# Batch 1's attention wholly inside unit 0, and batch 2's q^T by DMA transposes

## The chip, the cores and the metric

The kernel runs on one core of one Trainium2 chip. The metric is the device time of one execution in microseconds (us), lower is better. The kernel before took 335.55 us (median of 3 runs, 335.01 to 336.0). Where a text says "path", it means the instructions of TensorE (PE) in their order, since PE issues in order and nearly fills the span.

## What is computed

Per batch (8) and head (8) there are 1024 rows of 64 numbers. A Linformer attention is followed by a feed-forward layer with the larger of two products:

```python
k_proj = einsum('ks,bhsd->bhkd', E, k); v_proj = einsum('ks,bhsd->bhkd', F, v)   # 1024 -> 64 rows
attn = softmax(q @ k_proj^T / 8); x = attn @ v_proj        # per batch and head
x = x.transpose(0, 2, 1, 3).reshape(8192, 512)
out = maximum(x @ w1, x @ w2) @ w_out                      # 512 -> 1024 -> 512, float32
```

The inputs are float32 and are cast to float16 by the loads.

## The kernel before, in words

**Units.** Each batch makes two units of the feed-forward work, numbered 0 to 15. A unit has an "up" part (line 558, seven products p1, p2, p6, p5, p7, p3, p4 for each half of the features) and a "down" part (line 636, seven products of the same names). The matrices are multiplied in seven products of half size in place of eight, with sums and differences of operands made by VectorE (DVE): `step_s` (line 519) makes those of x and of g, `sub4` (line 475) those of the weights. A product that is kept is copied out of PSUM by `keep` (line 529), in unit 0's down part by DVE and elsewhere by ScalarE (ACT); `add` (lines 573 and 660) adds two of them.

**Order.** All instructions are in an order written out by hand. `slots` is a list of keys with a piece of work each, and `at_slot` hangs further steps behind a key. Batch 0's up part comes first (line 404); then unit 0's down part alone, in 14 pieces of 6 matmuls with keys ("P", 0, product, half). A list of 15 strings says which attention steps of batch 1 follow the pieces: string n stands behind piece n, and string 0 behind key (0, 19), ahead of the pieces. From unit 1 on, the down part of unit n and the up part of unit n + 1 alternate: some pieces of down, then key ("G", n, 0), some more pieces, then the up products ("U", n, 0, 0) to ("U", n, 0, 6) with a piece of down between each two; then the same with ("G", n, 1) and ("U", n, 1, i).

**Attention.** `step_kv` (line 180) projects k and v, ACT and DVE copy the results; `step_kpt` (line 211, copy on line 216) transposes k_proj on PE. q^T is made in one of two ways. `step_qt` (line 237) makes eight 128x128 transposes on PE, and DVE copies them out of PSUM in one instruction (line 242). `step_qt_dma` (line 249) has SyncE's DMA queue (SP) do it, 16 tiles a call. A batch has four groups (g, j): g is one of two sets of four heads, j one of two halves of the rows. A group's steps are the scores (`sc`, line 266, 16 small matmuls) with the exponential on ACT, the sums (`dn`, line 278, 8 matmuls) with a logarithm on ACT, the inverse (`in`, ACT) and the values (`at`, line 278, 16 matmuls), whose DVE multiplications write x^T (line 329 or 381). In unit 0 a group's steps are placed one by one. Later groups go through `step_group` (from line 333): behind key ("G", n, h) stand the sums and values of one group and the scores of the next.

**PSUM.** Unit 0's down part uses banks 0 and 1. The attention in unit 0 uses banks 2 and 3 by turns (`mm_bank`) for q^T and values, and two pairs of banks (`att_banks`) by turns for scores, sums and k_proj^T. `step_at` with `att=True` takes such a pair in place of banks 2 and 3. The up part of later units uses banks 2 and 3, too, and so do the scores in `step_group`.

**Loads.** k, v and q of a batch are loads of 1 MB each, which GpSimd's queue (POOL) issues in order into four buffers. A load waits on POOL until its buffer is free, and all behind it wait, too. `step_gate` (line 229) is a 1x1 copy on POOL which reads the result of a DMA transpose, so that the loads behind it on POOL start only once this has landed. Outputs are stored from four `o_sb` buffers by SP (line 651), in order with the DMA transposes.

**Batches before the change.** Of batch 1, the groups (0,0) and (1,0) and the scores of (0,1) are placed in unit 0; the group (0,1)'s sums and values and (1,1)'s scores stand behind ("G", 1, 0), (1,1)'s sums and values behind ("G", 1, 1). Batch 2's `step_kv` stands behind ("U", 1, 0, 1), its `step_kpt` behind ("U", 1, 0, 4), and four `step_qt` behind later up products of unit 1. Batches 3 to 7 use `step_qt_dma` at ("G", n, 0), a DMA transpose of k_proj, and the gate.

Of the kernel before, what the change touches and what calls it, by code (L numbers as in the profile page):

```python
# [16 lines left out]
def kernel(  # L17
# [14 lines left out]
    B, H, S, D = q.shape  # L32
# [27 lines left out]
    def mm_bank(dtype=FP32, n=None):  # L60
        if n is None:
            n = turn.pop(0)
            turn.append(n)
        return ps.tile([128, 512 if dtype == FP32 else 1024], dtype, tag=f"mm{n}", name="mm_ps")

    def att_banks(dtype=FP32):
        return ps.tile(
            [128, 2, 512 if dtype == FP32 else 1024], dtype, tag="att", bufs=2, name="att_ps"
        )
# [6 lines left out]
            name=nc.get_next_instruction_name(),  # L76
# [20 lines left out]
    def load_all(t, b, n, src):  # L97
        alloc(t, n)
        load(t, n, src, b, 0, H)
# [7 lines left out]
    tiles = {b: {} for b in range(B)}  # L107
# [180 lines left out]
    def values_into(t, g, j, at_ps):  # L288
        for z in range(2):
            tiles_into(  # L290
                lambda o: at_ps[o][:, z * W : (z + 1) * W], t["ex", g, j],
                lambda rows, hh: t["vp"][rows, 4 * g + hh, z, :],
            )

    def new_xt(t):
        t["xt"] = xpool.tile([128, NP2, 2, HALF], FP16, tag="xt", name="xt_sb")

    def x_out(t, g, j):
        return t["xt"][:, 2 * g : 2 * g + 2, :, j * W : (j + 1) * W]
# [15 lines left out]
        ld = t["ld", g, j]  # L315
        nc.scalar.activation(out=ld, in_=ld, func=ACTF.Exp, scale=-1.0)

    def step_at(t, g, j, att=False):
        if "xt" not in t:
            new_xt(t)  # L320
        ld = t.pop(("ld", g, j))
        if att:
            both = att_banks()
            at_ps = [both[:, o, :] for o in range(2)]
        else:
            at_ps = [mm_bank() for _ in range(2)]
        values_into(t, g, j, at_ps)
        for o in range(2):
            nc.vector.tensor_tensor(
                out=x_out(t, g, j)[:, :, o, :],  # L330
                in0=at_ps[o].rearrange("q (z n) -> q z n", z=2),
                in1=ld[:, o, None, :].broadcast_to([128, 2, W]),
                op=ALU.mult,
            )
# [121 lines left out]
    U = {(b, o): {"n": n, "b": b, "o": o, "t": tiles[b]} for n, (b, o) in enumerate(units)}  # L456
# [260 lines left out]
    t = tiles[0]  # L717
# [25 lines left out]
    step_dn(t, 1, 0)  # L743
    step_inv(t, 1, 0)
    step_at(t, 0, 0)
    step_dn(t, 1, 1)
    step_inv(t, 0, 1)
    step_kv(t, 4, 8, "v")
    step_inv(t, 1, 1)
    step_at(t, 1, 0)  # L750
    step_wd(0)

# [6 lines left out]

    def loads(b, *names):  # L760
        for n in names:
            b_ = b + (n == "k" and b < 3)
            if b_ < B:
                load_all(tiles[b_], b_, n, {"k": k, "v": v, "q": q}[n])

    slots = [
        (0, u0[0]), (None, f(step_at, 0, 1)), (1, u0[1]), (None, f(step_at, 1, 1)),
        (None, lambda: loads(1, "v", "q", "k")),
        (None, wd[1]), (2, u1[0]), (3, u1[1]), (4, u0[2]), (None, wt[0]), (5, u0[3]),
        (None, wd[2]), (None, wt[1]), (6, u1[2]), (7, u1[3]), (8, u0[4]), (9, u0[5]), (None, wd[3]),  # L770
# [30 lines left out]
    def at_slot(key, s, *a):  # L801
        steps.setdefault(key, []).append(lambda: s(*a))
# [11 lines left out]
    t = tiles[1]  # L814
    at_slot((0, 19), new_attn, t)
    at_slot((0, 19), lambda: turn.__setitem__(slice(None), [2, 3]))
    for n, x in enumerate((
        "kv", "", "kpt", "qt00 qt10", "", "sc00 sc10", "qt01", "qt11", "",
        "dn00 in00 dn10 in10", "", "", "at00 AT10 sc01", "", "",
    )):  # L820
        key = ("P", 0, (n - 1) // 2, (n - 1) % 2) if n else (0, 19)
        for name in x.split():
            if name[0] == "k":
                if name == "kpt":
                    at_slot(key, step_kpt, t, 0, H, True)
                else:
                    at_slot(key, step_kv, t)
                    at_slot(key, loads, 2, "v", "q")
            else:
                g, j = int(name[2]), int(name[3])  # L830
                s_ = {"qt": step_qt, "sc": step_sc,
                      "dn": step_dn, "in": step_inv, "at": step_at, "AT": step_at}[name[:2]]
                args = (4 * g, 4, 2 * j, 2 * j + 2) if name[:2] == "qt" else (g, j)
                at_slot(key, s_, t, *args, *([True] if name[:2] == "AT" else []))
                if name == "qt11":
                    at_slot(key, loads, 2, "k")
        if n in (1, 5):
            at_slot(key, step_t, 1, (0, 1) if n == 1 else (2, 3))
        if 6 <= n < 10:
            at_slot(key, sums_x, U[0, 1], ((2, 0, 1, 3)[n - 6],))  # L840


    t = tiles[2]
    at_slot(("P", 0, 6, 0), new_attn, t)
    at_slot(("U", 1, 0, 1), step_kv, t, 0, H, "kv", True)
    at_slot(("U", 1, 0, 1), loads, 3, "q", "v")
    at_slot(("U", 1, 0, 4), step_kpt, t, 0, H, True)
    for i, key in enumerate((("U", 1, 0, 5), ("U", 1, 1, 1), ("U", 1, 1, 3), ("U", 1, 1, 5))):
        at_slot(key, step_qt, t, 4 * (i % 2), 4, i // 2 * 2, i // 2 * 2 + 2, True)
    for b in range(3, B):  # L850
        t = tiles[b]
        n = 2 * b - 3
# [3 lines left out]
        at_slot(("U", n, 0, 1), step_kv, t, 0, H, "kv", True, True)  # L856
        at_slot(("U", n, 0, 6), step_gate, t)
        at_slot(("U", n, 0, 6), loads, b + 1, "k", "v", "q")
    groups = [(tiles[b], g, j) for b in range(1, B) for j in range(2) for g in range(2)][2:]
    none = (None, None, None)  # L860
    for i, (new, old) in enumerate(zip([*groups[1:], none], groups)):
        n, h = divmod(i + 2, 2)
        if new[0] is not None:
            at_slot(("G", n, h), lambda t=new[0], h=h: t.__setitem__("first", (h, 1 - h)))
        at_slot(("G", n, h), step_group, *new, *old)
        at_slot(("U", n, h, 0), step_later)
        at_slot(("U", n, h, 2), step_later)
# [59 lines left out]
```

## Time and profile before

| what | value |
|---|---|
| time of the profiled execution | 335.55 us |
| its span, first to last instruction | 333.8 us |
| median of the runs (3) | 335.55 us |
| lowest, highest | 335.01, 336.0 us |
| PE busy | 320.1 us (96%) |
| DVE busy | 242.2 us (73%) |
| ACT busy | 201.3 us (60%) |
| POOL busy | 37.0 us (11%) |
| granted PE clock, mean | 0.994 |

All times of instructions are us from the start of the span. A row of the timeline has the start, the time from the first start to the last end of the row, the engine, the line, what is written from what, and how many; in brackets stands the engine's idle time before it and what ended it. Matmuls are pipelined, so a row of them overlaps the next: a row's cost on the path is the distance from its start to the next row's start.

Where things stand in the span: unit 0's down part runs from 54.2 to 68.1, unit 1 from 68.1 to about 91, and from about 111.5 on each batch takes some 36 us.

### The profile page before, as it was taken

To read this page: it belongs to the slowest core of one execution; us is meant where nothing else is said; L and a number is where in the kernel's file an instruction comes from. 1 tells how busy PE (TensorE), PEld (TensorE's weight loads), DVE (VectorE), ACT (ScalarE), POOL (GpSimd) and SP (SyncE) were. 2 spreads that over 40 slices of the span, in tenths; PEclk is the share of its full clock that TensorE was granted. 3 is DMA by queue.
4 is the path that set the end of the run, shared out by engine and by line. 5 is a ranking of instruction groups with operands and counts; after the bars stand their busy time and mean duration, and the time that the engine had idled before them with its cause. 6 is when DMAs were issued, how large, how long until landed. Compare 5 with 4: busy or idle time off the path is not lost.

```text
span 333.8 us, 9067 instructions
## 1 busy us (share of the span) xinstructions
PE 320.1 (96%) x3884; PEld 250.2 (75%) x3884; DVE 242.2 (73%) x428; ACT 201.3 (60%) x359; POOL 37.0 (11%) x55
## 2 busy tenths in 40 slices
PE   8967999999999999999999999999999999999994
PEld 3542546777888788877888788878887888888883
DVE  1345598996886779677968779677967796969572
ACT  2362522565667677766777677767776777764541
POOL 8546002102000030002000020003000000000000
PEclk9997999999999999999999999999999999999999
DMA  7999999999911969975999899996999321212032
GB/s 152 200 200 174 207 207 202 202 228 218 221 38 44 211 87 211 221 181 94 170 244 218 145 131 232 206 195 88 215 218 201 73 97 33 94 33 96 32 128 94
DMA packets 70520, 52.09 MB, mean 156 GB/s; under 512 B 25296, under 2 KB 70352, under 8 KB 70480
## 3 DMA queue, kind: packets, MB, share of 16 engines
q0 software_dynamic: 29376, 28.31, 53.8%
q1 hardware_dynamic: 41104, 23.21, 28.2%
q8 instruction: 30, 0.49, 0.6%
q14 instruction: 10, 0.08, 0.1%
HBM read 57.15 MB, written 16.78 MB: 221 GB/s over the span
## 4 chain that ended last, share of the span: by engine, by line
PE 82%; DMA 7%; DVE 6%; issue 1%; POOL 1%; ACT 1%; DVEq 0%; POOLq 0%
PE mm_ps L636 40%; PE mm_ps L558 24%; PE mm_ps L404 4%; PE att_ps L180 3%; DMA big<-in_moe_w_dram 3%; PE att_ps L278 3%; PE mm_ps L266 3%; DMA k_sb<-in_k_dram 2%; PE mm_ps L440 2%; DVE gt_sb L573 1%; DMA kpt_sb<-kp_sb 1%; DVE qt_sb L242 1%; DVE o_sb L660 1%; DVE xt_sb L381 1%; POOL k_sb L102 1%
## 5 line engine op out<-in xcount | busy, mean ns | idle before, releaser
L529 ACT COPY p_sb<-mm_ps 128x512 f32<-128x512 f32 x172 | 97.2, 593 | 45.2 <-PE mm_ps L558 31.9
L636 PEld LDWEIGHTS <-big 128*128 128x128 f16 x768 | 73.5, 98 | 12.0 <-issue 3.5
L636 PE MATMUL mm_ps<-T_sb,big 128*128 128x256 f16 x576 | 77.9, 273 | 0.0
L573 DVE TENSOR_TENSOR gt_sb<-mm_ps,p_sb 128x512 f16<-128x512 f32 x56 | 38.5, 688 | 47.0 <-PE mm_ps L558 43.6
L558 PE MATMUL mm_ps<-big,big 128*128 128x256 f16 x336 | 50.4, 273 | 0.0
L558 PEld LDWEIGHTS <-big 128*128 128x128 f16 x448 | 43.8, 98 | 5.1
L636 PE MATMUL mm_ps<-wo_sb,gt_sb 128*128 128x256 f16 x256 | 42.9, 273 | 0.1
L636 PEld LDWEIGHTS <-gt_sb 128*128 128x128 f16 x384 | 35.6, 98 | 9.6 <-issue 5.4
L558 PEld LDWEIGHTS <-wd_sb 128*128 128x128 f16 x336 | 32.9, 98 | 4.1 <-issue 0.3
L558 PE MATMUL mm_ps<-xt_sb,wd_sb 128*128 128x256 f16 x224 | 33.6, 273 | 0.2 <-ACT ex_sb L355 0.2
L355 ACT ACTIVATE ex_sb<-mm_ps 128x512 f16<-128x512 f32 x50 | 27.2, 597 | 10.4 <-PE att_ps L278 7.0
L381 DVE TENSOR_TENSOR xt_sb<-att_ps,ld_sb 128x1024 f16<-128x1024 f32 x26 | 31.7, 1219 | 0.1
L660 DVE TENSOR_TENSOR o_sb<-mm_ps,p_sb 128x512 f32<-128x512 f32 x32 | 21.9, 685 | 11.0 <-PE mm_ps L636 7.5
L636 PE MATMUL mm_ps<-m_sb,xt_sb 128*128 128x256 f16 x128 | 24.4, 273 | 0.0
L608 ACT ACTIVATE gt_sb<-mm_ps 128x512 f16<-128x512 f32 x28 | 16.8, 600 | 8.7 <-PE mm_ps L558 8.7
L519 DVE TENSOR_TENSOR big<-gt_sb 128x1024 f16<-128x1024 f16 x32 | 21.9, 685 | 0.2
L576 DVE TENSOR_SCALAR gt_sb<-gt_sb 128x512 f16<-128x512 f16 (+1 forms) x56 | 20.4, 365 | 1.9
L636 PE MATMUL mm_ps<-T_sb,gt_sb 128*128 128x256 f16 x128 | 21.5, 273 | 0.0
L636 PE MATMUL mm_ps<-wo_sb,big 128*128 128x256 f16 x128 | 21.5, 273 | 0.0
L636 PEld LDWEIGHTS <-xt_sb 128*128 128x128 f16 x192 | 18.8, 98 | 2.2
L229 POOL COPY junk<-kpt_sb 1x1 f16<-1x1 f16 x5 | 1.1, 222 | 173.3 <-DMA kpt_sb<-kp_sb 173.3
L404 PE MATMUL mm_ps<-xt_sb,wd_sb 128*128 128x512 f16 x64 | 16.3, 400 | 3.0 <-DVE wd_sb L418 2.1
(88 smaller groups left out, 438.6 us busy)
## 6 DMA issues: line engine op xcount, KB each, us to landing
out_dram<-o_sb SPq DMA_DIRECT2D x63, 256.0 KB, 2.8
k_sb<-in_k_dram POOLq DMA_DIRECT2D x7, 1024.0 KB, 10.3
v_sb<-in_v_dram POOLq DMA_DIRECT2D x7, 1024.0 KB, 17.5
q_sb<-in_q_dram POOLq DMA_DIRECT2D x7, 1024.0 KB, 22.1
k_sb<-in_k_dram POOLq DMA_DIRECT2D x4, 256.0 KB, 7.1
q_sb<-in_q_dram POOLq DMA_DIRECT2D x4, 256.0 KB, 8.2
v_sb<-in_v_dram POOLq DMA_DIRECT2D x2, 512.0 KB, 12.8
big<-in_moe_w_dram POOLq DMA_DIRECT2D x8, 128.0 KB, 10.6
```

The source lines that it names most:

```text
L180: nc.tensor.matmul(out=kv_ps[r * KP : (r + 1) * KP, 0:n], lhsT=eft[:, i, c, :], rhs=t[w][:, h0:h1, c, :], start=(c == 0), stop=(c == NC - 1),)
L355: nc.scalar.activation(out=t["ex", g, j][:, e, :], in_=banks[e], func=ACTF.Exp, scale=scale)
L381: nc.vector.tensor_tensor(out=x_out(t, g, j).rearrange("q z o n -> q o z n"), in0=at_ps.rearrange("q o (z n) -> q o z n", z=2), in1=ld[:, ...
L404: nc.tensor.matmul(out=h_ps, lhsT=wd_sb[:, r, fb * 128 : (fb + 1) * 128], rhs=t["xt"][:, r, :, j * W : (j + 1) * W], start=(r == 0), stop= ...
L519: nc.vector.tensor_tensor(out=S(i), in0=x, in1=y, op=op)
L529: copy(out=x, in_=bank)
L558: nc.tensor.matmul(out=bank[:, m * W : (m + 1) * W], lhsT=w_[:, n_, (2 * d + m) * 128 : (2 * d + m + 1) * 128], rhs=a[:, n_, :], start=(n ...
L573: nc.vector.tensor_tensor(out=c_blk(j, c), in0=two(x), in1=two(y), op=ALU.add)
L576: nc.vector.tensor_scalar_max(ap, ap, 0.0)
L608: nc.scalar.activation(out=out, in_=in_, func=ACTF.Relu)
L636: nc.tensor.matmul(out=bank[:, i * CH : (i + 1) * CH], lhsT=a(c)[:, i * 128 : (i + 1) * 128], rhs=w_(c), start=(n is not None and m == (lo ...
L660: nc.vector.tensor_tensor(out=o_sb, in0=two(x), in1=two(y), op=ALU.add)
```

## The change

Batch 1's four groups are all placed in unit 0, each step in a spot of its own, and all values use banks 2 and 3. So ("G", 1, 0) and ("G", 1, 1) have no group of batch 1 any more; the latter keeps batch 2's first scores. Batch 2's `step_kv` moves to ("G", 1, 0), its `step_kpt` to ("U", 1, 0, 1), and its q^T is made by two `step_qt_dma` calls at ("G", 1, 0). A gate on q^T stands behind ("U", 1, 0, 6), and behind it the loads of batch 3's k, v and q. Before, that k was loaded in unit 0 (behind the transposes `qt11`), and q and v behind ("U", 1, 0, 1).

```diff
-    def step_at(t, g, j, att=False):
+    def step_at(t, g, j):
...
-        if att:
-            both = att_banks()
-            at_ps = [both[:, o, :] for o in range(2)]
-        else:
-            at_ps = [mm_bank() for _ in range(2)]
+        at_ps = [mm_bank() for _ in range(2)]
...
-            b_ = b + (n == "k" and b < 3)
+            b_ = b + (n == "k" and b < 2)
...
-        "kv", "", "kpt", "qt00 qt10", "", "sc00 sc10", "qt01", "qt11", "",
-        "dn00 in00 dn10 in10", "", "", "at00 AT10 sc01", "", "",
+        "kv", "", "kpt", "qt00 qt10", "", "sc00 qt01 qt11", "sc10", "dn00 in00", "sc01",
+        "at00 dn10 in10", "sc11", "at10 dn01 in01", "dn11 in11", "at01", "at11",
...
-                if name == "qt11":
-                    at_slot(key, loads, 2, "k")
...
     at_slot(("P", 0, 6, 0), new_attn, t)
-    at_slot(("U", 1, 0, 1), step_kv, t, 0, H, "kv", True)
-    at_slot(("U", 1, 0, 1), loads, 3, "q", "v")
-    at_slot(("U", 1, 0, 4), step_kpt, t, 0, H, True)
-    for i, key in enumerate((("U", 1, 0, 5), ("U", 1, 1, 1), ("U", 1, 1, 3), ("U", 1, 1, 5))):
-        at_slot(key, step_qt, t, 4 * (i % 2), 4, i // 2 * 2, i // 2 * 2 + 2, True)
+    at_slot(("G", 1, 0), step_kv, t, 0, H, "kv", True)
+    at_slot(("U", 1, 0, 1), step_kpt, t, 0, H, True)
+    at_slot(("G", 1, 0), step_qt_dma, t, 0, H // 2)
+    at_slot(("G", 1, 0), step_qt_dma, t, H // 2, H)
+    at_slot(("U", 1, 0, 6), step_gate, t, "qt")
+    at_slot(("U", 1, 0, 6), loads, 3, "k", "v", "q")
...
-    groups = [(tiles[b], g, j) for b in range(1, B) for j in range(2) for g in range(2)][2:]
+    groups = [(tiles[b], g, j) for b in range(2, B) for j in range(2) for g in range(2)]
     none = (None, None, None)
-    for i, (new, old) in enumerate(zip([*groups[1:], none], groups)):
-        n, h = divmod(i + 2, 2)
+    for i, (new, old) in enumerate(zip([*groups, none], [none, *groups])):
+        n, h = divmod(i + 3, 2)
```

More of the change, by code (lines that the diff above doesn't have):

```diff
@@ L831 @@
                 s_ = {"qt": step_qt, "sc": step_sc,
-                      "dn": step_dn, "in": step_inv, "at": step_at, "AT": step_at}[name[:2]]
-                args = (4 * g, 4, 2 * j, 2 * j + 2) if name[:2] == "qt" else (g, j)
-                at_slot(key, s_, t, *args, *([True] if name[:2] == "AT" else []))
-                if name == "qt11":
-                    at_slot(key, loads, 2, "k")
+                      "dn": step_dn, "in": step_inv, "at": step_at}[name[:2]]
+                at_slot(key, s_, t, *((4 * g, 4, 2 * j, 2 * j + 2) if name[:2] == "qt" else (g, j)))
         if n in (1, 5):
```

## The prediction, written before the changed kernel ran

> **What bounds the kernel now.** I read the busy times first, then the stretches, the chain of waits, and last the timelines of single engines between 54 and 94 us. The stretches (columns: busy time and instructions of PE, weight loads, DVE, ACT, POOL; clock, DMA share, GB/s):
>
> ```profile
> 60.00:76.00 16.00, 16.00 (x243) 12.46 (x239) 14.44 (x29) 9.31 (x16) 1.75 (x2) 1.00 1.19 218
> 76.00:94.00 18.00, 16.76 (x244) 13.80 (x242) 14.18 (x26) 11.12 (x21) 0.88 (x1) 1.00 0.99 194
> 94.00:111.50 17.50, 17.50 (x229) 15.05 (x227) 13.26 (x24) 12.68 (x24) 0.00 (x0) 1.00 0.28 78
> 111.50:147.50 36.00, 36.00 (x460) 29.73 (x457) 27.87 (x49) 25.54 (x48) 2.80 (x4) 1.00 0.97 176
> ```
>
> PE never rests in unit 0 or from 94 us on; only in unit 1 does it lose 1.24 us. The granted clock is 1.00 in all four. So a microsecond of PE work, or of PE waiting, between 58 and 94 us is a microsecond of the end. Second in line is DVE in unit 0, busy 14.4 of 16 us. PE's timeline:
>
> ```profile
> 63.57 0.41 PE L278 MATMUL att_ps<-ex_sb,ones 64*32 64x256 f16 x16
> 63.91 0.83 PE L636 MATMUL mm_ps<-T_sb,big 128*128 128x256 f16 x6
> ...
> 78.72 0.61 PE L237 MATMUL att_ps<-ident,q_sb 128*128 128x128 f16 x8
> 79.17 0.60 PE L636 MATMUL mm_ps<-T_sb,big 128*128 128x256 f16 x4
> ...
> 82.74 0.60 PE L558 MATMUL mm_ps<-xt_sb,wd_sb 128*128 128x256 f16 x4 [0.17 <-ACT ex_sb L355]
> ...
> 91.05 0.29 PE L278 MATMUL att_ps<-ex_sb,ones 64*32 64x256 f16 x8
> 92.32 0.41 PE L278 MATMUL att_ps<-ex_sb,vp_sb 64*32 64x256 f16 x16 [0.98 <-DVE qt_sb L242]
> ```
>
> A call of `step_qt` holds the path for 79.17 - 78.72 = 0.45 us. The values at 92.32 wait for DVE's last copy of q^T; by the rows at 109.06 and 109.17 they follow their sums after 0.11, so this wait costs 92.32 - 91.16 = 1.16 us.
>
> **A price for attention spots.** A feed-forward matmul takes 0.109 us of path (12 in 1.31). Twelve from 62.16 end at 63.47; the 16 sums then hold the path until 63.91: 0.44. In the same way 40 small matmuls took 0.78 (69.39 to 70.17) and 48 took 0.88 (65.88 to 66.76). All fit 0.22 per spot plus 0.11 per 8 matmuls. Spreading attention over more spots therefore costs 0.22 us each; a spot of 8 alone is in no row here, and by this line it is 0.33 (between 0.24, as at 14.80 to 15.04, and 0.44).
>
> **Added in unit 0.** Now, from 58.17 (piece 5) to 69.39 (("G", 1, 0)) the path has 60 + 12 feed-forward matmuls (7.86 us) and 3.34 us of attention: the scores 1.12 with a wait on a q^T copy, two `step_qt` 0.90, sums 0.44, values and scores 0.88. After: sc00 0.53 (it starts at 59.01 as now), qt01 and qt11 0.90, sc10 0.44, dn00 0.33, sc01 0.44, at00 with dn10 0.55, sc11 0.44, at10 with dn01 0.55, dn11 0.33, at01 0.44, at11 0.44; together 5.39.
>
> Waits come on top. I walked ACT and DVE through the new order with these rows. On ACT, an exponential of 128x1024 takes 1.02, a logarithm 0.60, an inverse 0.63. exp10 runs 61.5 to 62.5, dn00's logarithm ends at 63.06, so sc01, whose banks it frees, starts at 63.1, on time within 0.02. sc11 waits in the same way for dn10's logarithm, until 65.44 where PE comes at 65.43. That is 0.03 in all. On DVE the distance between starts counts: 0.60 for copies and additions of 512 float32 and for each multiplication of values, as the next rows have it, and 0.34 to 0.45 for sums.
>
> ```profile
> 66.09 0.69 DVE L660 TENSOR_TENSOR o_sb<-mm_ps,p_sb 128x512 f32<-128x512 f32 x1 [0.62 <-PE mm_ps L636]
> 66.69 0.68 DVE L660 TENSOR_TENSOR o_sb<-p_sb 128x512 f32<-128x512 f32 x1
> 67.29 1.28 DVE L329 TENSOR_TENSOR xt_sb<-mm_ps,ld_sb 128x512 f16<-128x512 f32 x2
> 68.49 1.28 DVE L329 TENSOR_TENSOR xt_sb<-att_ps,ld_sb 128x512 f16<-128x512 f32 x2
> ```
>
> From 59.47 DVE has p2's addition, two q^T copies, two weight differences (0.34, 0.41), p6's copy, two sums, p5's copy, a sum: 64.37. at00's multiplications wait for PE until 64.68, then with a sum and p7's copy 66.9; at10's start at 67.01 and end at 68.21; p3's two additions 69.41; at01's end at 70.69. at11 writes the banks that at01's free. PE is there at 69.85 and starts at 70.75: **a wait of 0.90**. No earlier one shows: at10 needs 65.96 and comes at 66.55, at01 needs 68.29 and comes at 68.75. Unit 0 thus takes 5.39 + 0.03 + 0.90 = 6.32 of attention against 3.34: **+2.98**. ("G", 1, 0) comes at about 72.4. The wait is not shown by any row; its ends are 0 (DVE's gaps ahead of at00's and at10's multiplications, 0.31 and 0.11, fall away and spots cost 0.05 less each) and 2.1 (two more operations of 0.60 get in front, as p3's two additions do). I take 0.90, since its sum is made of rows of the same instructions.
>
> **Removed in unit 1.** Four `step_qt`: 4 x 0.45 = 1.78, and 0.10 for a bank (86.24 to 86.34). The group at ("G", 1, 0): 0.78. At ("G", 1, 1) the path from 80.91 to 82.74 holds four feed-forward matmuls (0.44) and 1.39 more; after, only scores (0.44) and the wait for their exponential, which the row at 82.74 shows and which stays (0.34): 0.61 less. The wait at 92.32: 1.16. DVE loses four copies and two multiplications, so nothing takes that wait's place. Sum **4.43**. `step_kv` (1.94 with its change of form) and `step_kpt` (0.46) only move; k and v of batch 2 have landed by 59.4 and 65.4. Moving them makes p5 of the up part wait about 0.09 for an addition behind v_proj's copies on DVE.
>
> **Queues.** SP: batch 2's two DMA transposes stand behind unit 0's last store, whose ACT copy now comes behind the last inverse (69.56) and ends at about 70.6, and wait for q of batch 2.
>
> ```profile
> 55.40 0.88 POOL L102 DMA_DIRECT2D q_sb<-in_q_dram  x1
> ...
> 108.71 5.59 SPq L249 DMA_TRANSPOSE qt_sb<-q_sb  x2
> ```
>
> That load took 15.5 us to land, so 70.9. Issue at 71.1 (108.23 to 108.71 behind a store). Batch 3's two calls were complete 7.7 us after the first issue (2.07 until the second issue, 5.6 for it), batch 5's 7.4. So q^T is there at 78.7. The scores that wait for it come at 82.9: 4.2 us of cover. Stores behind the transposes are first wanted at 77.2, after both issues (76.7), and there are four buffers. POOL: the gate passes at 78.9; behind it wait k, v, q of batch 3. Behind the next gate the q load landed after 24.4 us (118.84 to 143.2): so 103.3, and SP wants it at 108.7 - 1.4 = 107.3, a cover of 4.0. Without either cover each microsecond late costs one. Ends for these two waits: nothing (no gain is possible, as PE's order does not change by them) and, with calls that don't overlap (3.47 + 6.0 + 6.0), 86.6 - 82.9 = 3.7. I take nothing, since ten calls in this trace landed in 4.3 to 6.0. Everything from batch 3 on keeps its order.
>
> A rule speaks against the change. The Trainium skill, "VectorE: DVE Perf Modes", section "The three transpose paths", gives 1309 ns for a 128x128 transpose by DMA against 390 ns by TensorE and says to use TensorE where PSUM will do. By it 32 tiles, one after another, would take an estimated 42 us and the scores would wait for 30. This trace has 16 tiles landing in 5.0 us (median), and the measurement decides.
>
> **Sum.** -4.43 + 0.09 + 2.98 = **-1.36**. The profiled execution took 335.55, the same as the median: 335.55 - 1.36 = **334.2 us** (-0.4%). Its own range is 333.7 to 334.8.
>
> **Rivals.**
> - *Better, 333.3.* The wait before at11 doesn't come. For it: DVE's chain has gaps that PE sets. Against: DVE is full from 59 to 74 already.
> - *No change, 335.4.* The packed unit 0 gives the gain back: the wait before at11 is 2.1 in place of 0.90, 334.2 + 1.2. For it: DVE is the engine with least room there, and 2.4 us of multiplications are moved into it. Against: every earlier value step has 0.4 us or more to spare, and behind at11 the backlog ends, as in unit 1 DVE loses 4.7 us (four copies at 0.60, two multiplications at 1.13).
> - *Slower, 337.9.* q^T of batch 2 comes too late for the scores at ("G", 1, 1). It decides once q^T lands more than 11.8 us after 71.1; with 3.7 us late the time is 334.2 + 3.7. For it: SP, the load of q and POOL stand in a row, and now one DMA result is awaited by PE after 11.8 us rather than DVE copies spread over the unit. Against: the ten calls in the trace, and no load is in flight beside them.
> - That the change doesn't do what it says is no rival of its own: 32 transposes less are 32 matmuls less on PE; if they weren't on the path, the time is the second rival's.
>
> **Chances.** Forecast 0.55, better 0.12, no change 0.20, slower 0.13. A change below 0.3% (1.0 us) can't be told from none. The forecast's range passes 334.5 in about 1 of 7 cases: faster 0.47 + 0.12 = 0.59, same 0.08 + 0.20 = 0.28, slower 0.13. The range runs from the better case to past the second rival: 333.1 to 336.0.
>
> **What will show it.** No line 237 after 61 us; PE's idle before the last values of unit 0 of about 0.9 with DVE's x^T as releaser; ("G", 1, 0) some 3 us later than now and the batch 3 stage 1.4 us earlier; no wait for q^T at the first scores of batch 2. I am wrong if PE waits in unit 0 for ACT, if that idle exceeds 2 us, or if a DMA transpose releases the scores.

## The result, and the profile after

The changed kernel took 332.84 us (median of 4 runs, 332.65 to 333.04), beside 335.72 us for the kernel before (4 runs, 335.01 to 336.0). The ratio is 0.9917 (95% interval 0.9900 to 0.9935). So it is faster, by 2.9 us, where 1.4 was forecast, and the median lies 0.26 us below the range. One run of after_nogate below (346.28 us) lies over 1.5% above the fastest of its kernel and is left out of that kernel's median and ratio. Of the profiled executions the one after took 332.65 us (span 330.9), the one before 335.55 us (span 333.8). From the multiplications of values on, line numbers of the changed kernel are four lower (325 for 329, 554 for 558, 632 for 636, 647 for 651).

The four stretches of the prediction, now of the changed kernel (busy time and instructions of PE, weight loads, DVE, ACT, POOL; clock, DMA share, GB/s):

```profile
60.00:76.00 16.00, 15.35 (x245) 9.84 (x244) 13.76 (x27) 9.94 (x15) 0.00 (x0) 1.00 1.10 202
76.00:94.00 18.00, 17.82 (x220) 14.91 (x218) 12.89 (x27) 11.49 (x23) 2.90 (x4) 1.00 1.03 179
94.00:111.50 17.50, 17.50 (x227) 14.03 (x225) 13.05 (x23) 12.13 (x23) 0.00 (x0) 1.00 0.83 179
111.50:147.50 36.00, 36.00 (x459) 29.75 (x459) 27.87 (x49) 25.48 (x48) 2.81 (x4) 1.00 0.98 176
```

PE's idle time has changed places: 1.24 us in unit 1 before, now 0.65 in unit 0 and 0.18 in unit 1. The load of batch 3's data has moved into the third stretch (DMA share 0.83, it was 0.28). PE's timeline shows the rows that answer to those of the prediction:

```profile
68.57 0.38 PE L632 MATMUL mm_ps<-T_sb,xt_sb 128*128 128x256 f16 x2
69.27 0.27 PE L278 MATMUL mm_ps<-ex_sb,vp_sb 64*32 64x256 f16 x1 [0.32 <-DVE xt_sb L325]
69.87 0.41 PE L278 MATMUL mm_ps<-ex_sb,vp_sb 64*32 64x256 f16 x15 [0.33 <-DVE xt_sb L325]
70.21 0.61 PE L632 MATMUL mm_ps<-wo_sb,gt_sb 128*128 128x256 f16 x4
...
82.00 0.41 PE L266 MATMUL mm_ps<-qt_sb,kpt_sb 64*32 64x256 f16 x16
...
83.14 0.60 PE L554 MATMUL mm_ps<-xt_sb,wd_sb 128*128 128x256 f16 x4 [0.18 <-ACT ex_sb L351]
...
90.01 0.29 PE L278 MATMUL att_ps<-ex_sb,ones 64*32 64x256 f16 x8
90.12 0.40 PE L278 MATMUL att_ps<-ex_sb,vp_sb 64*32 64x256 f16 x16
90.45 0.39 PE L632 MATMUL mm_ps<-wo_sb,gt_sb 128*128 128x256 f16 x2
```

The last value step of unit 0 (`at11`) stands twice for DVE's x^T, once for each of its two banks. The scores at 82.00 wait for nothing, the wait for their exponential at 83.14 has stayed, and the values at 90.12 follow their sums after 0.11: the old wait for the last copy of q^T is gone.

**Where the 2.9 us came from.** Two marks cut the span: the first matmul of batch 1's `step_kv` (line 180), up to which both kernels have the same instructions, and the first feed-forward matmul behind the values of batch 2's first group. I call the time between them "the stretch". Everything that the prediction summed up lies in it. PE's timeline at the two marks before:

```profile
52.32 0.40 PE L180 MATMUL mm_ps<-k_sb,eft 128*64 128x512 f16 x1
...
92.66 0.39 PE L636 MATMUL mm_ps<-wo_sb,gt_sb 128*128 128x256 f16 x2
```

After, the second mark is the row at 90.45 above, and the first is this one:

```profile
51.32 0.40 PE L180 MATMUL mm_ps<-k_sb,eft 128*64 128x512 f16 x1
```

| part | before | after | difference |
|---|---|---|---|
| start to first mark | 52.32 | 51.32 | -1.0 |
| the stretch | 40.34 (to 92.66) | 39.13 (to 90.45) | -1.21 |
| of it unit 0, piece 5 to ("G", 1, 0) | 11.22 | 14.37 | +3.15 |
| of it unit 1, from there on | 23.27 | 18.92 | -4.35 |
| PE's wait for k_proj^T of batch 4 | 0.60 | 0 | -0.6 |

Together -2.8 of -2.9. The stretch came within 0.15 us of what was forecast (-1.36). The other two parts were not in the forecast. The wait for k_proj^T before, in the timeline:

```profile
151.93 1.20 SPq L223 DMA_TRANSPOSE kpt_sb<-kp_sb  x1
...
155.94 0.41 PE L266 MATMUL mm_ps<-qt_sb,kpt_sb 64*32 64x256 f16 x16 [0.60 <-DMA kpt_sb<-kp_sb]
```

And the same place after:

```profile
149.72 1.20 SPq L223 DMA_TRANSPOSE kpt_sb<-kp_sb  x1
...
152.95 0.62 PE L266 MATMUL mm_ps<-qt_sb,kpt_sb 64*32 64x256 f16 x16
```

Issue and scores stand as far apart in the program as before, yet the transpose landed 4.0 us after its issue before and 2.7 after. The trace's list of DMA packets shows what lay beside the late one: the profile's list of queues has a line "q8 instruction" with 30 packets of 16 KB, which load instructions, about one microsecond each. One such instruction fetch started 1.16 us after the issue at 151.93, and packets of the transpose then took up to 1395 ns. In the other four transposes of k_proj of that profile none takes more than 173. In the profile after, the same fetch starts 4.08 us behind the issue.

### The profile page after: what moved, and what is told of

The parts are those of the page before. It is cut to its first block, busy times and chain, and to the rows that moved or that the text cites. A ratio compares the mean times of both kernels' runs of the same rounds, so it can differ in the third digit from the quotient of the medians.

```text
span 330.9 us, 9012 instructions
## 1 busy us (share of the span) xinstructions
PE 319.5 (97%) x3852; PEld 247.9 (75%) x3852; DVE 239.9 (73%) x426; ACT 201.4 (61%) x358; POOL 37.1 (11%) x56
## 4 chain that ended last, share of the span: by engine, by line
PE 87%; DMA 5%; DVE 4%; issue 1%; POOL 1%; ACT 0%; DVEq 0%; POOLq 0%
PE mm_ps L632 43%; PE mm_ps L554 25%; PE mm_ps L400 5%; PE att_ps L180 3%; DMA big<-in_moe_w_dram 3%; PE att_ps L278 3%; PE mm_ps L266 3%; DMA k_sb<-in_k_dram 2%; PE mm_ps L436 2%; DVE xt_sb L325 1%; DVE o_sb L656 1%; PE mm_ps L278 1%; DVE gt_sb L569 1%; POOL k_sb L102 1%; PE mm_ps L237 1%
## 5 line engine op out<-in xcount | busy, mean ns | idle before, releaser
L351 ACT ACTIVATE ex_sb<-mm_ps 128x512 f16<-128x512 f32 x48 | 26.1, 597 | 9.3 <-PE att_ps L278 7.0
L377 DVE TENSOR_TENSOR xt_sb<-att_ps,ld_sb 128x1024 f16<-128x1024 f32 x24 | 29.3, 1219 | 0.1
```

The costliest lines, as they stand in the source:

```text
L351: nc.scalar.activation(out=t["ex", g, j][:, e, :], in_=banks[e], func=ACTF.Exp, scale=scale)
L377: nc.vector.tensor_tensor(out=x_out(t, g, j).rearrange("q z o n -> q o z n"), in0=at_ps.rearrange("q o (z n) -> q o z n", z=2), in1=ld[:, ...
```

## Experiments

Two theories. **Theory A:** the change is worth what the stretch shows, -1.2 us, as forecast; the rest is a start-up that varies from execution to execution (the first mark) and, at batch 4, a collision of an instruction fetch with a transpose. The change moves that collision, because PE has 64 instructions (32 weight loads, 32 matmuls) less ahead of it. **Theory B:** the change itself is worth the whole 2.9 us. All kernels below, with the stretch and the waits of their profiled executions:

| kernel | stretch, us | PE's wait for k_proj^T | median, ratio to before (95%) |
|---|---|---|---|
| before_same | 40.33 | 0.3, batch 4 | 334.75, 0.9999 (0.9978 to 1.0020) |
| after_same | 39.13 | none | 333.19, 0.9952 (0.9931 to 0.9972) |
| after_third | 39.12 | 0.9, batch 6 | 333.78, 0.9964 (0.9942 to 0.9986) |
| pack_only | 41.26 | 0.9, batch 4 | 335.68, 1.0011 (0.9986 to 1.0035) |
| dma_only | 37.20 | 1.0, batch 6 | 332.38, 0.9909 (0.9876 to 0.9943) |
| before_shift | 40.34 | none | 333.68, one run |
| after_shift | 39.13 | 0.3, batch 4 | 334.11, one run |
| after_nogate | 47.29 | none | 342.09, 1.0232 (1.0159 to 1.0305) |
| after_at11_pair | 38.15 | 0.9, batch 6 | 333.63, 0.9937 (0.9914 to 0.9961) |
| dma_shift | 37.20 | 0.6, batch 6 | 331.96, 0.9919 (0.9889 to 0.9949) |
| dma_shift48 | 37.20 | none | 331.10, 0.9892 (0.9867 to 0.9917) |
| after_shift48 | 39.13 | none | 333.12, 0.9954 (0.9934 to 0.9974) |

### The kernel before and the changed one once more (before_same, after_same)

Nothing is edited in either.

> The kernel before, unchanged. Three marks: the start of batch 1's k and v projection (52.39 us in the profile before, 51.38 after), which no instruction of the change precedes; the first feed-forward matmul behind the values of batch 2's first group (92.66 and 90.45); and PE's wait for k_proj^T of batch 4 (0.60 and none). Theory A (the change is worth the 1.2 us between the first two marks; the first mark differs from execution to execution; the wait of 0.60 belongs to the place of PE's code fetch): the first mark falls anywhere from 51.3 to 52.5, the distance between the first two is 40.27 within 0.1, the wait stays. Theory B (the start-up belongs to the program, the change makes it earlier): the first mark is 52.3 to 52.5 again and the time is 335.4 to 335.9.

> The changed kernel, unchanged. Theory A: first mark from 51.3 to 52.5, not at 51.38 again but by chance; distance between the first two marks 39.07 within 0.1; no wait for k_proj^T of batch 4. Theory B: first mark 51.3 to 51.5 again, time 332.6 to 333.1.

The changed kernel gained 0.48% here, 1.6 us of 335.17 (the median of 29 runs of the kernel before), in place of 2.9. The stretch came out the same to 0.01 us in both kernels, while the first mark lay at 50.04 and 50.16, where the first pair of profiles had 52.32 and 51.32. Both lie even below the 51.3 to 52.5 that was expected for Theory A, and the 52.3 to 52.5 of Theory B did not come again. Two things move the mark. One is when batch 0's first loads have landed: PE waits for its v, 0.44 and 0.41 us in the profile before, 0.17 once in this one, and the first feed-forward matmul (line 404) starts at 26.37 and 25.43. The other is the clock. The kernel before, first profile, PE's timeline:

```profile
19.77 1.06 PE L180 MATMUL mm_ps<-v_sb,eft 128*64 128x256 f16 x16 [0.44 <-DMA v_sb<-in_v_dram]
...
22.28 1.06 PE L180 MATMUL mm_ps<-v_sb,eft 128*64 128x256 f16 x16 [0.41 <-DMA v_sb<-in_v_dram]
...
26.37 1.89 PE L404 MATMUL mm_ps<-xt_sb,wd_sb 128*128 128x512 f16 x4 [2.09 <-DVE wd_sb L418]
...
28.75 1.31 PE L404 MATMUL mm_ps<-xt_sb,wd_sb 128*128 128x512 f16 x4
```

The same kernel in before_same:

```profile
21.34 1.06 PE L180 MATMUL mm_ps<-v_sb,eft 128*64 128x256 f16 x16 [0.17 <-DMA v_sb<-in_v_dram]
...
25.43 1.04 PE L404 MATMUL mm_ps<-xt_sb,wd_sb 128*128 128x512 f16 x4 [2.09 <-DVE wd_sb L418]
...
26.74 1.04 PE L404 MATMUL mm_ps<-xt_sb,wd_sb 128*128 128x512 f16 x4
```

The same instructions behind the same wait of 2.09 us take 1.89 in one execution and 1.04 in the other. The granted clock of the first profile, from 25.93 to 29.34:

```profile
25.93:29.34 3.41, 2.97 (x22) 0.86 (x23) 0.76 (x2) 0.60 (x1) 3.41 (x5) 0.50 1.24 177
```

A clock of 0.50 for 3.41 us; in before_same and after_same there is no such stretch, and from the first feed-forward matmul to the first mark they take 24.61 us each instead of the 25.95 and 26.03 of the first pair: 1.3 to 1.4 us. In the first pair both executions had the half clock, so there the 1.0 us between the first marks lies ahead of the first feed-forward matmul (26.37 and 25.29). The Trainium skill, "TensorE: Matmul & The Clock Gate", section "Part 1: The HAM clock gate", tells of a half rate and of an activity window of 3413 ns that runs freely and does not start anew with a kernel; the 3.41 us and the coming and going of it here agree.

### The changed kernel a third time (after_third)

Nothing is edited.

> The changed kernel once more, unchanged, in more rounds, to settle its size: 0.9917 (0.9900 to 0.9935) in the first comparison of 4 against 4 runs, 0.9952 (0.9931 to 0.9972) of 10 against 29 in the second. If the change is worth 1.2 us in units 0 and 1 and some 0.6 for the missing wait at batch 4 (shown to go and come with PE's code fetch), the ratio is 0.9946, within 0.9935 to 0.9960; if the first comparison was right and the second disturbed, 0.992 or less.

0.9964, 1.2 us: just outside the 0.9935 to 0.9960 that was expected, though its interval reaches into it. In this profile batch 6 waited 0.9 us for k_proj^T (issued at 221.75, landed after 4.2 us, a fetch starting 2.14 us behind the issue). In the two other profiles of the same kernel that fetch stood 2.28 and 2.56 us behind, and the transpose took 2.7. So the changed kernel is at the edge of such a wait at batch 6, and paid it in one of these three executions.

### The two parts alone (pack_only, dma_only)

pack_only has the kernel before with batch 1's groups placed as in the change, and nothing else:

```diff
-        "kv", "", "kpt", "qt00 qt10", "", "sc00 sc10", "qt01", "qt11", "",
-        "dn00 in00 dn10 in10", "", "", "at00 AT10 sc01", "", "",
+        "kv", "", "kpt", "qt00 qt10", "", "sc00 qt01 qt11", "sc10", "dn00 in00", "sc01",
+        "at00 dn10 in10", "sc11", "at10 dn01 in01", "dn11 in11", "at01", "at11",
...
-    groups = [(tiles[b], g, j) for b in range(1, B) for j in range(2) for g in range(2)][2:]
+    groups = [(tiles[b], g, j) for b in range(2, B) for j in range(2) for g in range(2)]
...
-    for i, (new, old) in enumerate(zip([*groups[1:], none], groups)):
-        n, h = divmod(i + 2, 2)
+    for i, (new, old) in enumerate(zip([*groups, none], [none, *groups])):
+        n, h = divmod(i + 3, 2)
```

> One part alone: batch 1's four groups wholly in unit 0, batch 2's q^T by TensorE and all loads as before. Theory A: unit 0 takes 3.1 us more, unit 1 gets back 1.39 (the group's spots), and 0 to 1.16 of the wait for DVE's q^T copy: 0.6 to 1.8 us later than before at the second mark, so slower, some 336.3 (range 335.9 to 337.4). The wait of 0.60 in batch 4 stays as the number of PE instructions is that of before. Rival (the packing is what makes the change good, as it takes attention out of unit 1): not slower than before.

dma_only has the kernel before with q^T of batch 2 by DMA, the gate and the later loads; batch 1 stays as it was, and `step_kv` and `step_kpt` of batch 2 stay where they were:

```diff
-            b_ = b + (n == "k" and b < 3)
+            b_ = b + (n == "k" and b < 2)
...
-                if name == "qt11":
-                    at_slot(key, loads, 2, "k")
...
-    at_slot(("U", 1, 0, 1), loads, 3, "q", "v")
-    for i, key in enumerate((("U", 1, 0, 5), ("U", 1, 1, 1), ("U", 1, 1, 3), ("U", 1, 1, 5))):
-        at_slot(key, step_qt, t, 4 * (i % 2), 4, i // 2 * 2, i // 2 * 2 + 2, True)
+    at_slot(("G", 1, 0), step_qt_dma, t, 0, H // 2)
+    at_slot(("G", 1, 0), step_qt_dma, t, H // 2, H)
+    at_slot(("U", 1, 0, 6), step_gate, t, "qt")
+    at_slot(("U", 1, 0, 6), loads, 3, "k", "v", "q")
```

> The other part alone: batch 2's q^T by two DMA transposes behind key (G, 1, 0) with the gate and the loads behind it; batch 1's groups and batch 2's projections stay where they were before. Theory A: 1.78 + 0.10 + 1.16 = 3.04 us less in unit 1, nothing lost in unit 0, q^T landed at about 78.7 and wanted at 81.2; and as 64 PE instructions fewer stand ahead of batch 4, the wait of 0.60 goes as well: 331.5 to 332.8, faster than the changed kernel by about 1.5. Rival (without the packing the scores wait for q^T or the saving is lost to another wait): 333 or more.

The stretch decides: the packing alone costs 41.26 - 40.33 = 0.93 us, the DMA part alone gains 40.33 - 37.20 = 3.13. In the whole time packing can't be told from no change (335.68, below the 335.9 to 337.4 that was expected), and the DMA part is faster than the kernel before by 0.9%. Its wait at batch 4 is gone, as expected; one of 1.0 us at batch 6 came that was not. The two do not add: -3.13 + 0.93 = -2.20, and together they give -1.21. The wait of 0.98 for the last q^T copy goes with either part, since packing too removes work from DVE in unit 1 (pack_only keeps a wait of 0.3 for a q^T copy in its place), and it can be won only once. Next to the DMA part, packing therefore costs 39.13 - 37.20 = 1.93.

### Moving the instruction fetches (before_shift, after_shift)

32 matmuls of one column, whose results nobody reads, are added to PE's stream near the start, where PE waits for 2 us anyway. They move the places in the program at which the fetches fall, and leave all that follows as it is.

```diff
+    w_ps = mm_bank(n=turn[0])
+    for _ in range(32):
+        nc.tensor.matmul(
+            out=w_ps[0:32, 0:1], lhsT=ones16[:, 0:32], rhs=ones16[:, 0:1], start=True, stop=True
+        )
```

> The kernel before with 32 matmuls of one column more, put where PE idles for two us before the first feed-forward matmul; they compute nothing that is used, and shift each later instruction of PE by 64 places in its code. If the wait for k_proj^T of batch 4 belongs to a code fetch that lands within 1 to 2 us of that DMA transpose's issue (it did in the three profiles that have the wait there, 1.15, 1.27 and 1.87 us after the issue), the fetch now comes some 3.5 us earlier, before the issue, that transpose lands in 2.7 us and the wait of 0.3 to 0.9 is gone from batch 4 (it may arise at another batch). Rival (the wait comes from how batch 2's q^T is made or from the loads' times): the wait stays in batch 4, as nothing else is changed.

> The changed kernel with the same 32 matmuls, so that PE's code has again the places of the kernel before from batch 2 on. Code fetch theory: the fetch falls again some 1.2 us behind the issue of batch 4's k_proj^T, which lands in about 4 us, and the wait of 0.3 to 0.9 comes back. Rival (the change's new order of DMAs removed the wait): 2.7 us and no wait.

In the kernel before, the fetch moved from 1.16 us behind the issue of batch 4's transpose to 2.40 us ahead of it; the transpose landed in 2.7 us and the wait was gone. In the changed kernel it moved from 4.08 behind to 1.16 behind; the transpose landed in 3.6 us and a wait of 0.3 was there. The stretch stayed as it was in both. The wait comes and goes with the fetch, not with the change.

### The gate (after_nogate)

The changed kernel without the gate, its loads at the old places.

```diff
-            b_ = b + (n == "k" and b < 2)
+            b_ = b + (n == "k" and b < 3)
...
+                if name == "qt11":
+                    at_slot(key, loads, 2, "k")
...
-    at_slot(("U", 1, 0, 6), step_gate, t, "qt")
-    at_slot(("U", 1, 0, 6), loads, 3, "k", "v", "q")
+    at_slot(("U", 1, 0, 1), loads, 3, "q", "v")
```

> The changed kernel without the gate on q^T: batch 3's k is loaded in unit 0 behind the last q^T transposes, its q and v behind the second up product of unit 1, as before the change. It asks what the gate is worth. If loads in flight slow the DMA transposes, both calls land later than the 78.7 of the forecast: up to 4.2 us later costs nothing, beyond that each us is one us at the first scores of batch 2. Theory (the transposes share the 16 DMA engines with 1 MB loads, which alone take 5.0 to 5.5 us each there): q^T complete at about 84 to 86, a wait of 1 to 3 us, time 1 to 3 us above the changed kernel. Rival (the cover is enough or the loads don't touch the transposes): the same as the changed kernel within 0.4.

Both expectations were far too small: the time is 2.3% longer than before the change (three runs from 341.14 to 346.08), the stretch 8.2 us longer than with the gate. The timeline, SP and PE:

```profile
70.45 15.71 SPq L249 DMA_TRANSPOSE qt_sb<-q_sb  x2
86.26 9.27 SPq L647 DMA_DIRECT2D out_dram<-o_sb  x4
...
86.60 0.41 PE L266 MATMUL mm_ps<-qt_sb,kpt_sb 64*32 64x256 f16 x16 [4.17 <-DMA qt_sb<-q_sb]
...
98.30 0.41 PE L266 MATMUL mm_ps<-qt_sb,kpt_sb 64*32 64x256 f16 x16 [2.49 <-DMA qt_sb<-q_sb]
```

With loads in flight the two calls land 16.1 and 20.7 us after their issues; with the gate, 5.5 and 4.4. PE waits 6.7 us for them, SP's stores stand behind, and a half-clock stretch (87.16 to 90.57) follows PE's idle time. So the mechanism of the prediction's rival "slower" is real, and holding the loads back is what keeps it away. The edit takes the gate out and puts the loads back to their earlier places at once, so it prices the two together.

### The wait before `at11` (after_at11_pair)

`at11` of batch 1 takes the pair of banks that the scores use, and so need not wait for `at01`'s banks.

```diff
-        at_ps = [mm_bank() for _ in range(2)]
+        if (t is tiles[1], g, j) == (True, 1, 1):
+            both = att_banks()
+            at_ps = [both[:, o, :] for o in range(2)]
+        else:
+            at_ps = [mm_bank() for _ in range(2)]
```

> The changed kernel with the last values of unit 0 (group (1,1)) in a pair of attention banks, so that they don't wait for DVE to empty banks 2 and 3. In the profile after, their path cost from the end of the piece before (68.78) to the next feed-forward matmul (70.21) is 1.43, against 0.44 for such a spot without a wait. Theory: the distance between the two marks falls from 39.13 by 0.99 to 38.14, and the time by as much against the changed kernel (0.993 of the kernel before). Rival (DVE's backlog then makes the next step wait, batch 2's projection or the feed-forward's p6): less than half of it.

The stretch shortened by 0.98 us (39.13 to 38.15). That is the whole wait: nothing took its place. Its profile pays 0.9 at batch 6 again, so the time, 0.9937, can't be told from the changed kernel's by these runs.

### The DMA part with shifts (dma_shift, dma_shift48, after_shift48)

dma_only with 16 of the small matmuls, then with 48, and the changed kernel with 48 (the edit is that of before_shift, with another count).

> The version with batch 2's q^T by DMA and the gate, but batch 1's groups where they were before (3.1 us less between the two marks), with 16 of the small unused matmuls ahead of the first feed-forward matmul, so that PE's code fetches come 1.7 us earlier against the DMA transposes of k_proj^T: in the profile without them one fell 2.11 us behind that of batch 6, which then landed in 4.3 us in place of 2.7 and cost 1.0; the others lay 4.1 us behind or ahead of the issue. Code fetch theory: now 0.4 and 2.4 us behind at batches 6 and 4, where no wait was seen at 2.25 and more, so no wait at any batch; distance of the marks 37.2; ratio 0.9890 (0.9875 to 0.9905), about 1.9 us below the changed kernel. Rival (the fetch at 0.4 or 2.4 delays a transpose as well): ratio 0.9905 to 0.992.

Missed: the fetch at batch 6 moved from 2.11 to 1.20 us behind the issue, not out of the way. The wait fell from 1.0 to 0.6 only. One fetch moved 0.9 us and another 1.8 for the same 16 matmuls, so how far a fetch moves is not the same everywhere.

> The same as the version with 16 small matmuls at the start, but with 48. Fetch theory: in that version the code fetch lay 2.31 us behind the issue of batch 4's k_proj^T transpose and 1.19 us behind batch 6's, which came late by 1.2 us. 32 more matmuls moved the fetches of the kernel before and of the changed one by 3.2 to 3.6 us towards the start, so here they fall ahead of both issues by about 1 us or more: all five transposes land in 2.7 us, PE never waits for kpt_sb, and from 90 to 290 us the profile is 0.6 us shorter. The stretch from step_kv of batch 1 to the values of batch 2 stays at 37.20 us. Time: 331.4 us (330.5 to 332.3). Rival (the late transposes have another cause, and the instructions at the start shift them by chance): batch 4 or batch 6 waits 0.3 to 1.0 us again.

> The changed kernel with 48 small matmuls at the start. Fetch theory: with 32 of them the fetch lay 1.16 us behind the issue at batch 4 and 0.92 us ahead of it at batch 6; with 48 it is ahead of both (by about 0.6 and 2.7 us), so no transpose is late and PE never waits for kpt_sb. The stretch from step_kv of batch 1 to the values of batch 2 stays at 39.13 us. So this kernel and the DMA part alone with 48 differ by the packing of batch 1 alone, 39.13 - 37.20 = 1.9 us, and not by fetches. Time: 333.3 us (332.3 to 334.3). Rival: batch 4 or batch 6 waits again, or the two kernels differ by less than 1 us.

With 48, neither kernel has a wait for k_proj^T. Batch 6 in dma_only:

```profile
219.67 1.20 SPq L223 DMA_TRANSPOSE kpt_sb<-kp_sb  x1
...
224.02 0.41 PE L266 MATMUL mm_ps<-qt_sb,kpt_sb 64*32 64x256 f16 x16 [1.02 <-DMA kpt_sb<-kp_sb]
```

And in dma_shift48:

```profile
220.41 1.20 SPq L223 DMA_TRANSPOSE kpt_sb<-kp_sb  x1
...
223.56 0.62 PE L266 MATMUL mm_ps<-qt_sb,kpt_sb 64*32 64x256 f16 x16
```

The medians, from the same comparison, differ by 333.12 - 331.10 = 2.02 us; the stretches by 1.93. And the sum agrees with the times against the kernel before, which waited 0.3 and 0.6 us at batch 4 in its two profiles: -3.13 for the stretch and this wait make -3.5 to -3.7, and 0.9892 of 334.7 is -3.6 (-4.5 to -2.8); for the changed kernel -1.21 and the wait make -1.5 to -1.8, and 0.9954 is -1.5 (-2.2 to -0.9). dma_shift48 has the lowest median of all kernels here.

Over the 14 profiles there are 70 transposes of k_proj. Eight landed late (3.6 to 4.3 us), and in all eight a fetch started 1.16 to 2.14 us behind the issue. In the other 62 no fetch started between 0 and 2.2 us behind it.

## Why the prediction was wrong, point by point

**Theory A holds.** The mechanism and the sum for units 0 and 1 were right. Two things that the sum put at nothing were not: a change in the waits from batch 3 on, and a difference in the start. Point by point:

- *The spots.* 5.39 us of attention on PE's path in unit 0, without waits, were forecast. Measured: 14.37 less 7.86 of feed-forward work and 0.98 of waiting, 5.53. The price of 0.22 per spot and 0.11 per 8 matmuls held.
- *"A wait of 0.90" before at11.* From the row at 68.57 to that at 70.21 went 1.64 us; the two matmuls take 0.22 and an unhindered spot 0.44, so the wait was 0.98. DVE is what ends it, as forecast. DVE's timeline of the changed kernel:

```profile
66.13 1.29 DVE L325 TENSOR_TENSOR xt_sb<-mm_ps,ld_sb 128x512 f16<-128x512 f32 x2
67.33 0.68 DVE L656 TENSOR_TENSOR o_sb<-mm_ps,p_sb 128x512 f32<-128x512 f32 x1
67.93 0.68 DVE L656 TENSOR_TENSOR o_sb<-p_sb 128x512 f32<-128x512 f32 x1
68.53 1.28 DVE L325 TENSOR_TENSOR xt_sb<-mm_ps,ld_sb 128x512 f16<-128x512 f32 x2
70.43 1.29 DVE L325 TENSOR_TENSOR xt_sb<-mm_ps,ld_sb 128x512 f16<-128x512 f32 x2 [0.62 <-PE mm_ps L278]
```

  p3's two additions stand ahead of `at01`'s multiplications, as in the walk through DVE's order. Unit 0 came to +3.15 for +2.98.
- *Removed in unit 1.* -4.43 and +0.09, together -4.34, were forecast; -4.35 measured. Taken alone, the DMA part gained 3.13, where the four `step_qt` with their bank and the wait at 92.32 were priced at 1.78 + 0.10 + 1.16 = 3.04.
- *q^T in time.* SP and POOL in the changed kernel:

```profile
70.09 5.20 SPq L249 DMA_TRANSPOSE qt_sb<-q_sb  x2
...
78.03 0.26 POOL L229 COPY junk<-qt_sb 1x1 f16<-1x1 f16 x1 [22.75 <-DMA qt_sb<-q_sb]
78.55 0.88 POOL L102 DMA_DIRECT2D k_sb<-in_k_dram  x1 [0.25 <-issue]
```

  All forecast times stand 1.0 us lower here, as the first mark does: issue 71.1 (70.09), gate 78.9 (78.03), scores 82.9 (82.00). The cover is 4.0 us, 4.2 were forecast. q of batch 3, issued at 80.28, landed after 21.6 us, at 101.9, 4.6 ahead of SP's issue at 106.50; 4.0 were forecast. The 16-tile calls landed in 5.5 and 4.4 us, so the figure weighed in the prediction (the Trainium skill, "VectorE: DVE Perf Modes", section "The three transpose paths": 1309 ns for a 128x128 transpose by DMA), taken one tile after another, doesn't hold for them. On line 237 no instruction starts after 59.2, as forecast.
- *"Everything from batch 3 on keeps its order."* **This step failed.** The order is kept, but not the times: a PE stream that is 64 instructions shorter moves its instruction fetches, and batch 4's k_proj^T transpose is no longer hit. That is -0.6 in the profiled pair, and in the third profile of the changed kernel +0.9 at batch 6 instead. The wait stood in the profile of before (0.60 at 155.94, with a transpose that took 4.0 us where the others took 2.7); it was read as belonging to the kernel, and was not asked about.
- *The base.* The sum was set against one profiled execution whose start to the first mark took 52.32 us. **This failed too.** In the nine profiles without added matmuls the first mark lies between 50.04 and 52.52, a spread of 2.5 us that the start makes, not the change. In the first pair of profiles it gave the changed kernel 1.0 us, by luck and more than the margin of 0.26 by which the range was missed. Of the runs without a profile it isn't known where their first mark lies, so that the same holds for all four of the first comparison is likely, but not shown. The three longer comparisons of the changed kernel, with and without shift, give 0.9952, 0.9964 and 0.9954, or -1.6, -1.2 and -1.5 us, each to about 0.7 us. The forecast of -1.36 lies in all three intervals; that it comes this close is in part chance, since these totals hold the gains and losses at the fetches too, which the sum did not have. Like for like is the stretch, -1.21. The first interval (0.9900 to 0.9935) holds none of the three ratios: its four runs lay within 0.4 us, while the same kernel later ran from 331.25 to 335.05.
- *The rivals.* "Better", the wait before `at11` left away, is what after_at11_pair makes; its worth was 0.98, for 0.90. "No change" and "slower" did not come; the latter comes without the gate, at 342.09, since the transposes are stretched far more than the bound of 3.7 us for calls that don't overlap.

**Open.** How a fetch delays a transpose is settled in part only. In the trace the end of a transpose is told by 16 semaphore updates. In five of the eight late ones (a fetch 1.16 to 1.87 us behind the issue) packets of the transpose took over 1000 ns, and all 16 updates came late, after 3.5 us. In the three with a fetch 2.10 to 2.14 us behind no packet took that long: 15 updates came within 2.7 us, as in a transpose that isn't hit, and only the last one came late, at 4.2 to 4.3. So there one part of sixteen is held up, and PE waits for that one. Why a fetch holds it so long is not shown. That the first mark depends on the loads and on the clock was read from profiles; no experiment changed either by itself.

## What to carry to other kernels

Cut two profiles at marks up to which the kernels are identical: what differs ahead of the first mark is not the change's own, what differs behind the last is not what a sum between the marks has priced, and a gain near the size of these differences needs repeated comparisons. When a change makes a bundle of two, price each against the other: here one part paid 3.1 us and the other gave 1.9 of it back. And ask of each wait in the profile before whether it is a property of the order or a chance meeting of a DMA with an instruction fetch, which any edit of the instruction stream can move.

## What the runs showed of the hardware that was not expected

- DMA transposes beside loads: two 16-tile calls landed in 5.5 and 4.4 us with no load in flight, and in 16.1 and 20.7 us with the loads of batch 3 beside them. The 158 such calls of all profiles with no load in flight took 4.3 to 6.4. The work that stood behind them on SP, four stores, came late as well.
- Instruction fetches are DMA traffic: 30 packets of 16 KB in a span, about 1 us each. A k_proj^T transpose that is hit 1.16 to 2.14 us behind its issue took 3.6 to 4.3 us instead of 2.7 (eight of eight).
- Around a wait of 2.09 us the clock fell to 0.50 for 3.41 us in some executions, and not in others of the same kernel; it cost 1.3 us.
